# A decode step of two attention and two feed-forward layers: one K transfer of each layer in uneven rows

## The chip, the core and the metric

The kernel runs on one core of a Trainium2 chip. A core has five engines with their own instruction streams: PE (TensorE, the matrix unit), DVE (VectorE), ACT (ScalarE), POOL (GpSimd) and SP (SyncE), which here only issues transfers. Sixteen DMA engines move data from the chip's memory into the core's on-chip memory, which has 128 rows (partitions). Matmul results go to a separate accumulator memory, PSUM; its tiles are called `pS` and `pO` here.

The metric is the device time of one execution in microseconds, the median over several runs.

## The reference

One token goes through attention, a feed-forward block, and both once more with the same weights and the same caches. Cut to what is computed:

```python
def _A_ref(x, k_cache, v_cache, wq, wo):          # x: 1 x 1 x 512
    B, Sq, D = x.shape
    H, Dh = 32, 128                                # caches: 1 x 32 x 4096 x 128
    q = (x @ wq).reshape(B, Sq, H, Dh)             # then heads first
    scores = jnp.einsum("bhqd,bhkd->bhqk", q, k_cache) * (Dh ** -0.5)
    p = _softmax(scores, axis=-1)
    o = jnp.einsum("bhqk,bhkd->bhqd", p, v_cache)
    return o.reshape(B, Sq, H * Dh) @ wo           # heads back in place first

def _B_ref(x, w1, b1, w2, b2):                     # 512 -> 1376 -> 512
    h = jnp.einsum("bsd,df->bsf", x, w1) + b1
    h = _gelu(h)
    return jnp.einsum("bsf,fd->bsd", h, w2) + b2

x = A_x
x = x + _A_ref(_layernorm(x, axis=-1), A_k_cache, A_v_cache, A_wq, A_wo)
x = x + _B_ref(_layernorm(x, axis=-1), B_w1, B_b1, B_w2, B_b2)
x = x + _A_ref(_layernorm(x, axis=-1), A_k_cache, A_v_cache, A_wq, A_wo)
x = x + _B_ref(_layernorm(x, axis=-1), B_w1, B_b1, B_w2, B_b2)
return x
```

All numbers are float32. Each cache holds 67 MB, and each has to be read in both layers, but for the parts that the kernel keeps on the chip between them.

## The kernel before

The 32 heads are treated as `G = 8` groups of `J = 4` heads. The host lays the caches out so that the K of one group, `in_k[g]`, is a block of 128 rows of 16,384 numbers (64 KB a row, 8.39 MB in all), and V likewise. A block is cut along the row into `C = 8` pieces of `NC = 2048` numbers, one for each eighth of the sequence.

**One group.** K is transferred, and `scores` takes it piece by piece: four matmuls for each piece (one for each head), 32 in all, added up in `pS`. `exponentials` and `weights` make the softmax: maximum on DVE, exponential on ACT, a transpose on PE. V is transferred, and `values` runs its 32 matmuls into `pO`. `head_out` multiplies by the group's part of `wo`, and `next_queries` makes the query of the next group from its part of `wq`; both parts come in one transfer of 2 MB (`pair`).

**Where things lie.** One tile, `arena`, holds all that is transferred. Three places of 8.39 MB each, `RING`, take K and V of the groups in turn, so a transfer may begin when the matmuls that read the earlier tenant of its place are done. `PAIR` holds the two weight parts.

**Two layers.** Layer 1 goes through the groups 0 to 7 and ends with the feed-forward block `mlp`. Layer 2 goes back from the groups whose K and V are still on the chip: first two groups that are partly there, and then, in the loop over `n` from 2 to 7, groups 5 to 0. In the last group of each layer K goes in two halves (`HALVES`) and V in four pieces (`LAST`).

**What sets the order.** `load` issues each transfer on SP and keeps it in program order; `matmul` keeps PE's order. SP issues a transfer as soon as its waits are over. The sixteen DMA engines work through what SP has issued. Each transfer counts up one of eight semaphores, `DMAHW0` to `DMAHW7`, taken in turn by SP's transfers and by ACT's three small ones at the start (`xcol`, `b1c`, `b2c`); a transfer also waits for the one before it on its semaphore, where nothing else has waited for that already.

**What the change touches.** `blocks` (line 251) issues the transfers of a K or V and yields its pieces; its argument `pieces` says in how many transfers. It is called with one piece for the whole block, `((0, C),)`, at line 289 for layer 1 (with `g` the group) and at line 361 for layer 2 (with `n`). The profile shows all transfers of `load` at line 70, and all matmuls but the transposes at line 74. A K transfer is shown there as `arena<-in_k`.

Of the kernel before, what the change touches and what calls it, by code (L numbers as in the profile page):

```python
# [23 lines left out]
C = 8  # L24
# [5 lines left out]
NC = 4 * U  # L30
# [12 lines left out]
HALVES = ((0, 4), (4, 8))  # L43
# [7 lines left out]
def decode_layers(ctx: ExitStack, tc: tile.TileContext, x, k, v, w, w1, b1, w2, b2, out):  # L51
    nc = tc.nc
# [12 lines left out]
    def at(first, n):  # L65
        return arena[:, first : first + n]

    def load(first, src):
        t = at(first, src.shape[-1])
        tc.keep_in_program_order(nc.sync.dma_start(t, src))  # L70
        return t

    def matmul(*a, **kw):
        tc.keep_in_program_order(nc.tensor.matmul(*a, **kw))  # L74

    def quarters(first):
        return [at(first + U * j, U) for j in range(4)]

    def part(src, g, a, b):
        return src[g][:, NC * a : NC * b]  # L80

    def of_w(row, i, n):
        return w[row][:, NC * i : NC * (i + n)]

    def by_four(t):
        return t.rearrange("p (j n) -> p j n", j=4)


    wq_t = by_four(load(SHARED, of_w(1, 0, 1)))
    b1c, b2c = ctile("b1c", FB), ctile("b2c", 4)  # L90
    xcol = ctile("xcol", 4)
# [71 lines left out]
    def scores(z, c, kt):  # L163
        for j in range(J):
            matmul(pS[32 * j : 32 * j + C, :], z[:, j, C - 1 - c : 2 * C - 1 - c], kt[j],
                   start=(c == 0), stop=(c == C - 1))

    def exponentials(sc, nsc):
        nc.vector.tensor_reduce(mx[:, 0:1], pS, axis=AX.X, op=ALU.max)  # L169
        mt, m, bias = small("mt", 32), small("m"), small("bias", 32)  # L170
        nc.vector.transpose(mt, mx)  # L171
        nc.vector.tensor_reduce(m, mt[:, :C], axis=AX.X, op=ALU.max)
        nc.vector.tensor_scalar(mb[:, :C], m.to_broadcast([P, C]), nsc, None, op0=ALU.mult)  # L173
        nc.vector.transpose(bias, mb)  # L174
        p = at(SCRATCH, U)
        nc.scalar.activation(p, pS, AF.Exp, bias=bias[:, 0:1], scale=sc, accum_out=ls[:, 0:1])  # L176
        return p

    def weights(p):
        for b in range(4):  # L180
            tc.keep_in_program_order(nc.tensor.transpose(  # L181
                pT[:, b].rearrange("p j r -> p (j r)"), p[:, P * b : P * (b + 1)], ident))
        pt = work.tile([P, J, C, 4], F32, name="pt")
        nc.vector.tensor_copy(pt, pT[:, :, :, :C].rearrange("p b j c -> p j c b"))  # L184
        lt, l, lr, rl = small("mt", 32), small("l"), small("lr", 32), small("rl")
        nc.vector.transpose(lt, ls)  # L186
        nc.vector.tensor_reduce(l, lt[:, :C], axis=AX.X, op=ALU.add)
        nc.vector.tensor_copy(lb, l.to_broadcast([P, 32]))
        nc.vector.transpose(lr, lb)
        nc.vector.reciprocal(rl, lr[:, 0:1])  # L190
        return pt, rl

    def values(i, pt, vt, c):
        for j in range(J):
            matmul(pO[32 * j : 32 * j + 4, :], pt[:, j, c, :], vt[j],
                   start=(i == 0), stop=(i == C - 1))

    def head_out(rl, wt):
        ot = at(SCRATCH, U)
        nc.vector.transpose(ot, pO)  # L200
        o, on = small("o", 4), small("on", 4)
        own = at(SCRATCH, 4 * 129).rearrange("p (b q) -> p b q", q=129)[:, :, :P]
        own = own.rearrange("p b (d q) -> p d b q", q=32)[:, :, :, 0]
        nc.vector.tensor_reduce(o, own, axis=AX.X, op=ALU.add)  # L204
        nc.vector.tensor_scalar(on, o, rl, None, op0=ALU.mult)  # L205
        for d in range(4):
            for j in range(J):
                matmul(pS[32 * j : 32 * j + 1, :P], on[:, d : d + 1], wt[:, d, P * j : P * (j + 1)],
                       start=(d == 0), stop=(d == 3))
        return of_32(turned(pS), 4)  # L210
# [31 lines left out]
    def load_w1(first, a, b):  # L242
        load(first + W1C * a, w1[:, W1C * a : W1C * b])

    def load_w2(first, a, b):
        load(first + U * a, w2[:, U * a : U * b])
# [1 line left out]
    def in_rows(first, n, rows):  # L248
        return [at(first + n * i, n) for i in range(rows)]

    def blocks(src, g, home, pieces=((0, C),)):
        for a, b in pieces:
            load(home + NC * a, part(src, g, a, b))
            for c in range(a, b):
                yield c, quarters(home + NC * c)

# [16 lines left out]
    def next_queries(n, xs, negm, wt):  # L273
        for c in range(4):
            query_block(c, xs, wt)
        return queries(n, negm)

    def add_up(acc, own):
        t = small("acc", 4)
        nc.vector.scalar_tensor_tensor(t, own, 1.0, acc, op0=ALU.mult, op1=ALU.add)  # L280
        return t
# [4 lines left out]
    for g in range(G):  # L286
        final = g == G - 1
        k_home, v_home = RING[2 * g % 3], RING[(2 * g + 1) % 3]
        for c, t in blocks(k, g, k_home, HALVES if final else ((0, C),)):
            scores(z, c, t)  # L290
        pt, rl = weights(exponentials(sc, nsc))
        if final:
            wo_t = by_four(load(PAIR, of_w(g % 2, g, 1)))
        for c, t in blocks(v, g, v_home, LAST if final else ((0, C),)):
            values(c, pt, t, c)
            if g == G - 2:
                for j in range(J):
                    i = 4 * c + j - KEPT_V // U
                    if i >= 0:
                        nc.scalar.copy(pK[i], t[j])  # L300
        if final:
            for i in range(3):
                load_w1(SHARED, i, i + 1)
            own = head_out(rl, wo_t)
            load_w1(SHARED, 3, 4)
        else:
            pair = load(PAIR, of_w(g % 2, g, 2))
            acc = add_up(acc, head_out(rl, by_four(pair[:, :NC])))
            wq_t = by_four(pair[:, NC:])
            z = next_queries(g + 1, xs, negm, wq_t)  # L310
# [7 lines left out]
    g = G - 2  # L318
# [26 lines left out]
    for i, first in enumerate([SHARED + 8 * U, SHARED + 9 * U] + [PAIR + U * j for j in range(4)]):  # L345
        t = at(first, U)
# [11 lines left out]
    for n in range(2, G):  # L358
        g, final = G - 1 - n, n == G - 1
        k_home, v_home = homes[(2 * n - 1) % 3], homes[2 * n % 3]  # L360
        for c, t in blocks(k, g, k_home, HALVES if final else ((0, C),)):
            scores(z, c, t)
        pt, rl = weights(exponentials(sc, nsc))
        if final:
            wo_t = by_four(load(PAIR, of_w(g % 2, g, 1)))
        for c, t in blocks(v, g, v_home, LAST if final else ((0, 6), (6, 8)) if n == 2 else ((0, C),)):
            values(c, pt, t, c)
        if final:
            for a, b in HALVES_W1:
                load_w1(A_AT, a, b)  # L370
            for a, b in W2_AT_END:
                load_w2(A_AT + 11 * U, a, b)
            own = head_out(rl, wo_t)
        else:
            pair = load(PAIR, of_w(g % 2, g - 1, 2))
            acc = add_up(acc, head_out(rl, by_four(pair[:, NC:])))
            z = next_queries(n + 1, xs, negm, by_four(pair[:, :NC]))
# [47 lines left out]
```

## Time and profile before

| | |
|---|---|
| median of 3 runs | 683.48 us (683.07 to 687.48) |
| the profiled execution | 684.24 us |
| its span, from the first instruction to the last | 682.5 us |
| read from the chip's memory in the span | 286.14 MB, 419 GB/s |
| TensorE clock granted, mean | 0.772 |
| matmuls of `scores` (`pS<-arena,zq`) | 1024, 144.1 us busy, 725 ns each |
| matmuls of `values` (`pO<-arena,pt`) | 1024, 146.5 us busy, 734 ns each |
| idle time of TensorE ahead of `scores`, mostly until a K lands | 160.3 us |

How to read the profile: the page begins with each engine's busy time and share of the span (PEld is TensorE's weight load, which overlaps PE). Then come 40 equal slices of the span: a digit is the busy share of a slice in tenths, DMA is the mean of the core's sixteen DMA engines, and GB/s is what they moved. The queues follow: q1 is what SP issues, q10 what ACT issues, q8 and q14 fetch instructions. The chain is followed back from the last instruction: at each step to what released it. In it, "another core or an unknown queue" stands for a wait that no instruction of the core ended; in the middle of this kernel's layers the operation that comes behind it is one that reads transferred data. All times in the views are in microseconds from the start of the span. The clock granted is a share of TensorE's full clock.

### The profile page before, as it was taken

To read this page: it belongs to the slowest core of one execution; us is meant where nothing else is said; L and a number is where in the kernel's file an instruction comes from. 1 tells how busy PE (TensorE), PEld (TensorE's weight loads), DVE (VectorE), ACT (ScalarE), POOL (GpSimd) and SP (SyncE) were. 2 spreads that over 40 slices of the span, in tenths; PEclk is the share of its full clock that TensorE was granted. 3 is DMA by queue.
4 is the path that set the end of the run, shared out by engine and by line. 5 is a ranking of instruction groups with operands and counts; after the bars stand their busy time and mean duration, and the time that the engine had idled before them with its cause. 6 is when DMAs were issued, how large, how long until landed. Compare 5 with 4: busy or idle time off the path is not lost.

```text
span 682.5 us, 7552 instructions
## 1 busy us (share of the span) xinstructions
PE 351.9 (52%) x3440; PEld 99.5 (15%) x3440; DVE 83.6 (12%) x346; ACT 21.9 (3%) x47; POOL 3.6 (1%) x17
## 2 busy tenths in 40 slices
PE   1543663545524655156565878625525643366554
PEld 0111110111111111012012222111111110111112
DVE  1011100111001100111012121110011101111012
ACT  0010000000000000001000010000000000000000
POOL 0000000000000000000000000000000000000000
PEclk9968766797678866787768898886577866877778
DMA  9999999999999999999999999999999999999995
GB/s 369 431 430 443 442 443 435 424 437 430 427 430 408 450 430 431 434 419 434 428 397 337 375 433 423 427 443 447 438 431 404 458 431 438 424 419 429 427 416 225
DMA packets 10976, 286.63 MB, mean 420 GB/s; under 512 B 1728, under 2 KB 1728, under 8 KB 3008
## 3 DMA queue, kind: packets, MB, share of 16 engines
q1 hardware_dynamic: 10512, 286.14, 98.1%
q8 instruction: 27, 0.44, 0.3%
q10 hardware_dynamic: 432, 0.01, 0.0%
q14 instruction: 5, 0.04, 0.0%
HBM read 286.14 MB, written 0.00 MB: 419 GB/s over the span
## 4 chain that ended last, share of the span: by engine, by line
PE 39%; DMA 26%; another core or an unknown queue 25%; DVE 6%; ACT 1%; issue 1%; SPq 0%; ACTq 0%; DVEq 0%
PE pO L74 20%; PE pS L74 18%; DMA arena<-in_v 10%; DMA arena<-in_w 8%; DMA arena<-in_k 7%; DVE arena L200 1%; ACT arena L176 1%; PE pO L181 1%; DVE mx L169 1%; DMA xcol<-in_x 1%; DVE on L205 0%; DVE mb L173 0%; DVE mt L171 0%; DVE o L204 0%
## 5 line engine op out<-in xcount | busy, mean ns | idle before, releaser
L74 PE MATMUL pS<-arena,zq 128*8 128x512 f32 x1024 | 144.1, 725 | 160.3 <-DMA arena<-in_k 159.1
L74 PE MATMUL pO<-arena,pt 128*4 128x512 f32 x1024 | 146.5, 734 | 84.6 <-DMA arena<-in_v 83.8
L74 PEld LDWEIGHTS pS<-arena,zq 128*8 128x8 f32 x1024 | 30.0, 102 | 263.8 <-issue 248.3
L74 PEld LDWEIGHTS pO<-arena,pt 128*4 128x4 f32 x1024 | 28.1, 98 | 193.0 <-issue 186.6
L169 DVE TENSOR_REDUCE mx<-pS 128x1 f32<-128x512 f32 x16 | 11.1, 692 | 294.0 <-PE pS L74 294.0
L200 DVE STREAM_TRANSPOSE arena<-pO 128x512 f32<-128x512 f32 x16 | 11.5, 717 | 225.7 <-PE pO L74 225.7
L181 PE MATMUL pO<-ident,arena 128*128 128x128 f32 x64 | 13.7, 351 | 44.7 <-ACT arena L176 44.7
L176 ACT ACTIVATE arena<-pS,bias,sc 128x512 f32<-128x512 f32 x16 | 12.4, 777 | 544.6 <-DVE bias L174 544.6
L74 PE MATMUL pO<-arena,xs 128*2 128x128 f32 (+1 forms) x576 | 24.4, 307 | 9.5 <-DVE xs L126 8.3
L74 PE MATMUL pS<-arena,on 128*1 128x128 f32 x512 | 16.9, 272 | 21.2 <-DVE on L205 21.2
L181 PEld LDWEIGHTS pO<-ident,arena 128*128 128x128 f32 x64 | 8.8, 174 | 58.8 <-ACT arena L176 53.8
L74 PEld LDWEIGHTS pS<-arena,on 128*1 128x1 f32 x512 | 11.6, 83 | 36.6 <-DVE on L205 36.1
L74 PEld LDWEIGHTS pO<-arena,xs 128*2 128x2 f32 x576 | 14.5, 87 | 13.1 <-issue 9.2
L74 PE MATMUL pS<-arena,gelu_g 128*1 128x128 f32 x176 | 8.6, 355 | 7.2 <-DVE gelu_g L235 4.3
L119 DVE STREAM_TRANSPOSE turned<-pS 128x128 f32<-128x128 f32 x18 | 5.7, 317 | 30.5 <-PE pS L74 30.5
L74 PEld LDWEIGHTS pS<-arena,gelu_g 128*1 128x1 f32 x176 | 4.8, 102 | 11.5 <-DVE gelu_g L235 5.6
L119 DVE STREAM_TRANSPOSE turned<-pO 128x128 f32<-128x128 f32 x16 | 5.1, 316 | 5.5 <-PE pO L74 4.7
L186 DVE STREAM_TRANSPOSE mt<-ls 128x32 f32<-128x32 f32 x16 | 3.4, 211 | 17.4 <-ACT arena L176 17.4
L184 DVE COPY pt<-pO 128x128 f32<-128x128 f32 x16 | 4.3, 267 | 2.0 <-PE pO L181 2.0
L173 DVE TENSOR_SCALAR mb<-m,nsc 128x8 f32<-128x8 f32 x16 | 3.7, 231 | 0.6
L205 DVE TENSOR_SCALAR on<-o,rl 128x4 f32<-128x4 f32 x16 | 3.7, 229 | 0.6
L159 DVE SCALAR_TENSOR_TENSOR zq<-turned,negm 128x4 f32<-128x4 f32 x16 | 3.6, 226 | 0.5
(58 smaller groups left out, 54.6 us busy)
## 6 DMA issues: line engine op xcount, KB each, us to landing
arena<-in_w SPq DMA_DIRECT2D x13, 2048.0 KB, 36.1
arena<-in_k SPq DMA_DIRECT2D x5, 4096.0 KB, 46.0
arena<-in_v SPq DMA_DIRECT2D x2, 4096.0 KB, 24.1
arena<-in_w SPq DMA_DIRECT2D x6, 1024.0 KB, 14.8
arena<-in_v SPq DMA_DIRECT2D x3, 2048.0 KB, 28.5
arena<-in_v SPq DMA_DIRECT2D x1, 6144.0 KB, 32.2
arena<-in_v SPq DMA_DIRECT2D x4, 1024.0 KB, 31.5
arena<-in_w SPq DMA_DIRECT2D x4, 688.0 KB, 30.4
```

Of the source, the lines that this page charges most:

```text
L74: tc.keep_in_program_order(nc.tensor.matmul(*a, **kw))
L119: nc.vector.transpose(t, src[:, :P])
L159: nc.vector.scalar_tensor_tensor(z[:, :, C - 1], of_32(qt, J, 1), negm, of_32(qt, J), op0=ALU.mult, op1=ALU.add)
L169: nc.vector.tensor_reduce(mx[:, 0:1], pS, axis=AX.X, op=ALU.max)
L173: nc.vector.tensor_scalar(mb[:, :C], m.to_broadcast([P, C]), nsc, None, op0=ALU.mult)
L176: nc.scalar.activation(p, pS, AF.Exp, bias=bias[:, 0:1], scale=sc, accum_out=ls[:, 0:1])
L181: tc.keep_in_program_order(nc.tensor.transpose(pT[:, b].rearrange("p j r -> p (j r)"), p[:, P * b : P * (b + 1)], ident))
L184: nc.vector.tensor_copy(pt, pT[:, :, :, :C].rearrange("p b j c -> p j c b"))
L186: nc.vector.transpose(lt, ls)
L200: nc.vector.transpose(ot, pO)
L205: nc.vector.tensor_scalar(on, o, rl, None, op0=ALU.mult)
```

## The change

A new helper, `load_uneven`, issues one block of rows as three transfers: rows 0 to 111, rows 112 to 119 and rows 120 to 127. `blocks` gets an argument `uneven`; with it, every piece but the first goes through the new helper. It is used once in each layer: for K of group 1 in layer 1, and for K of `n == 3` (group 4) in layer 2. These K now go in two halves of 4.19 MB, the first as one transfer of 128 rows, the second in the three. A row of a half is 8192 numbers, 32 KB. The change is described as one by which eight DMA engines carry two rows more than the others: 112 rows are seven for each of sixteen engines, and the two transfers of 8 rows are one row each for eight of them, and the same eight in both.

```diff
+    def load_uneven(first, src):
+
+        t = at(first, src.shape[-1])
+        for a, b in ((0, 112), (112, 120), (120, 128)):
+            tc.keep_in_program_order(nc.sync.dma_start(t[a:b], src[a:b]))
...
-    def blocks(src, g, home, pieces=((0, C),)):
+    def blocks(src, g, home, pieces=((0, C),), uneven=False):
         for a, b in pieces:
-            load(home + NC * a, part(src, g, a, b))
+            (load_uneven if uneven and a else load)(home + NC * a, part(src, g, a, b))
             for c in range(a, b):
                 yield c, quarters(home + NC * c)
...
-        for c, t in blocks(k, g, k_home, HALVES if final else ((0, C),)):
+        for c, t in blocks(k, g, k_home, HALVES if final or g == 1 else ((0, C),), g == 1):
...
-        for c, t in blocks(k, g, k_home, HALVES if final else ((0, C),)):
+        for c, t in blocks(k, g, k_home, HALVES if final or n == 3 else ((0, C),), n == 3):
```

What moves, on SP at the start of layer 1. Each row is a transfer, its size and the semaphores that it waits for; the second row is K of group 0, the fifth K of group 1, then come V of group 1, the weights, and K and V of group 2. Before:

```order
L70 DMA arena<-in_w 128x2048
L70 DMA arena<-in_k 128x16384
L70 DMA arena<-in_v 128x16384 [waits DMAHW1_49,PE_49]
L70 DMA arena<-in_w 128x4096
L70 DMA arena<-in_k 128x16384
L70 DMA arena<-in_v 128x16384 [waits DMAHW4_49,DMAHW0_49,PE_49]
L70 DMA arena<-in_w 128x4096 [waits DMAHW6_49,PE_49]
L70 DMA arena<-in_k 128x16384 [waits DMAHW5_49,DMAHW2_49]
L70 DMA arena<-in_v 128x16384 [waits DMAHW7_49,DMAHW3_49,PE_49]
```

After:

```order
L70 DMA arena<-in_w 128x2048
L70 DMA arena<-in_k 128x16384
L70 DMA arena<-in_v 128x16384 [waits DMAHW1_49,PE_49]
L70 DMA arena<-in_w 128x4096
L70 DMA arena<-in_k 128x8192
L77 DMA arena<-in_k 112x8192 [waits DMAHW0_49]
L77 DMA arena<-in_k 8x8192
L77 DMA arena<-in_k 8x8192 [waits DMAHW2_49]
L70 DMA arena<-in_v 128x16384 [waits DMAHW4_49,DMAHW3_49,PE_49]
L70 DMA arena<-in_w 128x4096 [waits DMAHW6_49,PE_49]
L70 DMA arena<-in_k 128x16384 [waits DMAHW5_49]
L70 DMA arena<-in_v 128x16384 [waits DMAHW2_49,DMAHW1_49,DMAHW7_49,DMAHW0_49,PE_49]
```

One K row has become four. With three more transfers in the turn of the eight semaphores, the waits for `DMAHW2` and `DMAHW3` (those of ACT's `b1c` and `b2c`) have moved forward: from K and V of group 2 to the second 8-row transfer and to V of group 1. The wait for `DMAHW0`, which the first weights count up, has moved from V of group 1 to the 112 rows.

On SP in layer 2, from K of `n == 3` on. Before:

```order
L70 DMA arena<-in_w 128x4096 [waits DMAHW2_49,DMAHW1_49,Activation_49]
L70 DMA arena<-in_k 128x16384
L70 DMA arena<-in_v 128x16384 [waits DMAHW6_49,PE_49]
L70 DMA arena<-in_w 128x4096 [waits DMAHW1_49,PE_49]
L70 DMA arena<-in_k 128x16384 [waits DMAHW7_49,DMAHW0_49]
```

After:

```order
L70 DMA arena<-in_w 128x4096 [waits DMAHW5_49,DMAHW4_49,Activation_49]
L70 DMA arena<-in_k 128x8192
L77 DMA arena<-in_k 112x8192
L77 DMA arena<-in_k 8x8192 x2
L70 DMA arena<-in_v 128x16384 [waits DMAHW1_49,PE_49]
L70 DMA arena<-in_w 128x4096 [waits DMAHW4_49,DMAHW2_49,PE_49]
L70 DMA arena<-in_k 128x16384 [waits DMAHW3_49]
```

The added transfers wait for nothing here, and V waits for as many things as before.

On PE, the scores of group 1 in layer 1: the queries, the 32 matmuls of `scores` and the transposes behind them. Before:

```order
L74 MATMUL pO<-arena,xs 2x128 x16
L74 MATMUL pS<-arena,zq_92 8x512 [waits DMAHW7_49,DVE_49]
L74 MATMUL pS<-arena,zq_92 8x512 x31
L181 MATMUL pO<-ident,arena 128x128 [waits Activation_49]
L181 MATMUL pO<-ident,arena 128x128 x3
```

After:

```order
L80 MATMUL pO<-arena,xs 2x128 x16
L80 MATMUL pS<-arena,zq_92 8x512 [waits DMAHW7_49,DVE_49]
L80 MATMUL pS<-arena,zq_92 8x512 x15
L80 MATMUL pS<-arena,zq_92 8x512 [waits DMAHW2_49,DMAHW1_49,DMAHW0_49]
L80 MATMUL pS<-arena,zq_92 8x512 x15
L187 MATMUL pO<-ident,arena 128x128 [waits Activation_49]
L187 MATMUL pO<-ident,arena 128x128 x3
```

The first sixteen matmuls now wait for the first half alone, and the other sixteen for all three transfers of the second half.

## The prediction

> **What bounds the kernel now.** I read the page first: the shares of the engines, the 40 slices of the DMA engines, the queues and the chain.
>
> ```profile
> span 682.5 us, 7552 instructions
> ...
> PE 351.9 (52%) x3440; PEld 99.5 (15%) x3440; DVE 83.6 (12%) x346; ACT 21.9 (3%) x47; POOL 3.6 (1%) x17
> ...
> DMA  9999999999999999999999999999999999999995
> GB/s 369 431 430 443 442 443 435 424 437 430 427 430 408 450 430 431 434 419 434 428 397 337 375 433 423 427 443 447 438 431 404 458 431 438 424 419 429 427 416 225
> ...
> q1 hardware_dynamic: 10512, 286.14, 98.1%
> q8 instruction: 27, 0.44, 0.3%
> ...
> PE 39%; DMA 26%; another core or an unknown queue 25%; DVE 6%; ACT 1%; issue 1%; SPq 0%; ACTq 0%; DVEq 0%
> ```
>
> TensorE is busy for half of the span. The sixteen DMA engines are full in all slices but the last, and queue q1, which SP feeds, has 98.1% of them. The chain gives PE the largest share, but a chain counts a matmul as work even where the next one waits for data anyway. So I asked next for the busy time by stretch: the two around the first K transfer to be split, one behind them, and most of layer 2.
>
> ```profile
> core 0: us, PE busy (x) PEld busy (x) DVE busy (x) ACT busy (x) POOL busy (x), PEclk, DMA share, GB/s
> 12.00:56.00 44.00, 20.47 (x132) 4.53 (x132) 2.75 (x12) 2.15 (x3) 0.00 (x0) 0.84 1.00 429
> 58.00:100.00 42.00, 21.66 (x176) 5.30 (x164) 3.68 (x16) 0.87 (x2) 0.00 (x0) 0.67 1.03 442
> 100.00:144.00 44.00, 22.04 (x216) 6.43 (x220) 5.87 (x21) 0.87 (x2) 0.00 (x0) 0.73 1.00 430
> 466.00:630.00 164.00, 85.69 (x784) 23.65 (x784) 18.45 (x70) 3.47 (x8) 0.00 (x0) 0.72 1.00 429
> ```
>
> A share of 1.00 at 429 to 430 GB/s is a ceiling: 430 / 16 = 26.9 GB/s for each DMA engine. (The 442 beside a share of 1.03 is an effect of where a stretch is cut.) One group of a layer is K and V of 8.39 MB each and 2.1 MB of weights, 18.9 MB, or 43.9 us at that rate. The chain in order of time shows the same period; here is one group, and then the end.
>
> ```profile
> 59.15 11.27 another core or an unknown queue
> 70.56 9.47 PE pS L74 x64
> 80.05 0.70 DVE mx L169
> ...
> 83.85 5.93 another core or an unknown queue
> 89.92 10.02 PE pO L74 x64
> ...
> 133.49 8.73 PE pO L74 x64
> ...
> 510.28 9.76 PE pS L74 x64
> ...
> 645.01 31.12 DMA arena<-in_w
> 676.17 3.21 PE pS L74 x56
> ```
>
> From one V's matmuls (89.92) to the next (133.49) pass 43.6 us, the 43.9 us of the bytes. The gaps of 11.27 and 5.93 us are TensorE waiting for a landing. The kernel ends 6.3 us after the last weights land (676.17 to 682.5). How deep the queue is, SP's own rows tell:
>
> ```profile
> 9.10 0.46 SPq L70 DMA_DIRECT2D arena<-in_k  x1
> 35.28 0.33 SPq L70 DMA_DIRECT2D arena<-in_v  x1
> ...
> 59.63 0.38 SPq L70 DMA_DIRECT2D arena<-in_k  x1
> 80.04 0.33 SPq L70 DMA_DIRECT2D arena<-in_v  x1
> ...
> 449.83 0.38 SPq L70 DMA_DIRECT2D arena<-in_k  x1
> ```
>
> The V issued at 80.04 is used from 133.49, 53.4 us later; its own 8.39 MB take 19.5 us, so 33.9 us of other transfers stand ahead of it. Therefore nothing that happens on SP or TensorE within some 30 us matters, and the time is the time of the slowest DMA engine: each works down its own share of every transfer, and only the drain at the end of a layer makes them wait for each other.
>
> **The change, part by part.**
>
> *Halving the transfer.* TensorE may begin on the first half 9.7 us earlier and has about 4.7 us less to do once the whole K is there. This frees SP's next V earlier, into a queue 33.9 us deep: worth 0. If that cover were gone it would be worth up to 4.7 us in each layer.
>
> *Six more issues on SP,* three in each layer, at 0.33 to 0.46 us: 2.4 us in all. SP waits far longer than that, so they cost 0:
>
> ```profile
> SPq L70 <- DMA arena<-in_w: 227.7, 16, 35.4
> ```
>
> *Waits that the new semaphore order brings.* By the order shown above, the second 8-row transfer of layer 1 now waits for semaphore 2 and the V behind it for semaphore 3. These are the first ones that the ACT queue's small loads use, b1c and b2c.
>
> ```profile
> 1.16 0.46 ACTq L93 DMA_DIRECT2D b1c<-in_b  x1
> 1.65 0.45 ACTq L94 DMA_DIRECT2D b2c<-in_b  x1
> ...
> b1c<-in_b ACTq DMA_DIRECT2D x1, 5.5 KB, 24.3
> b2c<-in_b ACTq DMA_DIRECT2D x1, 2.0 KB, 44.7
> ```
>
> They land at 1.16 + 24.3 = 25.5 and 1.65 + 44.7 = 46.4 us. So the V goes out at 46.4 instead of 35.28. Behind it on SP stand weights and the K that went out at 59.63, so nothing else is held. The K that is split lands at about 70.5 (its matmuls start at 70.56), so 24 us of queue are still ahead of the V: 0. If the cover were gone the price would be 11.1 us, once. In layer 2 the added transfers bring no wait of their own.
>
> *The uneven rows.* This is the only term on the path. A row of the half is 32 KB: 32,768 B / 26.9 GB/s = 1.22 us of one engine. Evenly spread, the half costs every engine 8 rows, 9.7 us. After the change the 112 rows cost 7 rows, 8.5 us, and eight engines carry two rows more. What a transfer of only 8 rows costs these eight, no row of before shows, since all transfers on q1 have 128 rows. The bounds:
> - Low: the rate belongs to the engine, wherever it writes. Two rows cost 2.4 us; the eight engines end at 8.5 + 2.4 = 10.9 us, 1.2 us late, and the other eight 1.2 us early.
> - High: the rate belongs to the place written. In every transfer before, a sixteenth of the destination took in a sixteenth of 430 GB/s, never more. If eight adjacent rows are such a sixteenth, then one 8-row transfer takes 8 x 1.22 = 9.7 us on whichever engines, the two 19.5 us, and the eight engines end at 28.0 us, 18.3 us late.
>
> I take two sixteenths for eight adjacent rows: 4.9 us for an 8-row transfer, 9.7 us for both, end at 18.3 us, 8.5 us late. It is nearer to the high end, because the one thing that the rows of before do show of 8 rows of destination is 26.9 GB/s for 8 rows together, while an engine with its neighbours writing into the same few rows is shown nowhere.
>
> The Trainium skill has a rule for this that speaks against the change: SBUF — State Buffer, Door 1: The DMA port swizzle, says that four adjacent partitions share one of sixteen ports at about 27 GB/s, so eight adjacent ones reach two ports. By its figure the two transfers would cost 9.6 us, and the sum below would stand; by a rate of the engine alone it would be that of the first rival. No row of this trace can show it, since full transfers use all partitions. And on which engines: the Trainium skill, DMA: Bandwidth & Descriptors, Why a DMA increments its semaphore by 16 and not by 1, puts an 8-row transfer on the eight lowest-numbered engines; the profile does not name engines.
>
> *What of this reaches the end.* Some engines are late already, since instruction fetches fall on them: 27 on q8 take 0.3% of sixteen engines' span, 0.003 x 16 x 682.5 / 27 = 1.2 us each. If the other eight engines had all the 13 or 14 of a layer, the latest of them would have two, 2.4 us; if the same eight, the lead is 0. I take the middle, 1.2 us. So a layer ends 8.5 - 1.2 = 7.3 us later. The drain at the end of each layer makes all wait for the slowest, so the two layers add.
>
> **Sum.** 2 x 7.3 = 14.6 us; the other parts 0. The profiled execution took 684.24 us (the span and 1.74 us around it), 0.76 us above the median of the three runs, 683.48. Against the median: 698.1 us, 2.1% slower. This case's own range is 693 to 705: low, with a lead of three fetches, 3.6 us, 683.5 + 2 x 4.9; high, where the engines whose usual rows these are write there as well (five rows share the rate of one instead of four, 2 x 1.2 us more in each layer) and the lead is 0, 683.5 + 2 x 10.9.
>
> **The rivals.**
> 1. *The rate is the engine's, and the late engines are the other eight* (not slower). Place: the drain at the end of each layer. The eight get 1.2 us more each layer, the late ones 1.2 us less: 683.5 - 2.4 = 681.1 us. For it: 26.9 GB/s on each of sixteen, with nothing in the rows to say that the destination sets it, and fetches that do make engines unequal. Against it: fetches are worth only 1.2 us each, so the others may not be behind at all. It decides if an 8-row transfer takes less than about 1.8 us on its engines: then two rows more are at most the lead of 2.4 us and a little.
> 2. *The rate is the engine's, and the eight are those that are late already.* 2 x 1.2 us more: 685.9 us. The same rows speak for it.
> 3. *The change does not do what it says,* and the 16 rows spread over all sixteen engines, or the lag is taken up before the drain: 683.5 us. Against it: a queue that is never empty gives a late engine no time to catch up.
> 4. *Eight adjacent rows are one sixteenth.* 18.3 us late in each layer, less 1.2: 683.5 + 34.2 = 717.7 us.
>
> **How the numbers follow.** Chances: the forecast 0.54, rival 1 0.22, rival 2 0.10, rival 3 0.08, rival 4 0.06. A measurement of this kernel can tell about 1%, 6.8 us, from no change. Rivals 1 to 3 lie within it, 0.40. Slower by over 1% are the forecast and rival 4, 0.60, less 0.02 for a forecast that comes out small: 0.58. Faster by over 1% needs 6.8 us, which no row offers: 0.02. The range reaches from rival 1, with 0.3 us of spread, 680.8, to the upper part of the forecast, 705; it leaves out rival 4 and a tenth of the forecast, about 0.12.
>
> **What would show it.** For the forecast: the first matmuls of the split K's second half start some 8 us later than 70.56 and 510.28 against the bytes ahead of them; the moved GB/s fall below 400 in the slices around 50 to 75 and 490 to 515 us; the last weights' matmuls start near 691 (676.17 + 14.6) instead of 676.17. Against it: the rate stays at 430 there, and all landings keep their distance of 43.9 us. The halving is right if TensorE begins the first half early and V's start does not move; the new wait is right if V goes out at 46 us and its matmuls still start near 90, plus the lag. I am wrong above all if a few rows can be written by many engines at full rate.

## The result and the profile after

The changed kernel takes 717.53 us (median of 6 runs, 716.11 to 721.33) beside 684.46 us for the kernel before (6 runs): the ratio is 1.0473, with a 95% interval of 1.0446 to 1.0501. It is 4.7% slower; forecast were 698.1 us and a range up to 705.

The page of the changed kernel, the span, the DMA engines' busy tenths, what they moved, and SP's queue:

```profile
span 714.3 us, 7560 instructions
...
DMA  9999999999999999999988999999999999999995
GB/s 411 412 409 318 235 414 457 416 437 434 426 441 417 447 434 419 440 409 439 425 352 308 387 443 431 417 319 234 413 443 440 423 433 434 438 426 417 434 410 206
...
q1 hardware_dynamic: 10832, 286.14, 97.7%
```

The DMA engines are as busy as before and move the same 286.14 MB, but twice the rate falls: to 318 and 235 GB/s in the fourth and fifth slice (54 to 89 us), and to 319 and 234 in two slices of layer 2 (464 to 500 us). Those are the two places where the uneven halves go. Elsewhere the rate is about that of before. So a DMA engine can be busy and slow at once, and the busy share does not show it; the GB/s beside it do.

The same stretches of layer 1, as busy times with DMA share and GB/s at the end of each row, before:

```profile
58.00:72.00 14.00, 2.60 (x52) 1.15 (x44) 1.02 (x4) 0.00 (x0) 0.00 (x0) 0.63 1.02 441
72.00:84.00 12.00, 9.09 (x64) 2.31 (x56) 2.38 (x10) 0.87 (x2) 0.00 (x0) 0.78 1.01 437
```

and after:

```profile
58.00:72.00 14.00, 6.59 (x80) 1.96 (x70) 1.02 (x4) 0.00 (x0) 0.00 (x0) 0.88 1.03 261
72.00:84.00 12.00, 0.00 (x0) 0.00 (x0) 0.00 (x0) 0.00 (x0) 0.00 (x0) 0.52 1.06 169
```

The first stretch is mostly the 112 rows, the second the two 8-row transfers. Both are slow: 261 and 169 GB/s. (A packet is counted in the stretch in which it starts, so where the share is above 1.00 the GB/s is too high by about that factor.) The forecast had only the second one slow.

TensorE's instructions after, in order of time: start, length, and in brackets the idle time ahead and what ended it.

```profile
62.11 5.30 PE L80 MATMUL pS<-arena,zq 128*8 128x512 f32 x32 [2.82 <-DMA arena<-in_k]
86.05 5.28 PE L80 MATMUL pS<-arena,zq 128*8 128x512 f32 x32 [18.63 <-DMA arena<-in_k]
...
105.17 5.09 PE L80 MATMUL pO<-arena,pt 128*4 128x512 f32 x24 [10.44 <-DMA arena<-in_v]
```

The first half of K is there at 62, the second at 86, and V's matmuls start at 105.17 instead of 89.92: layer 1 is 15.3 us late from here on. The span grew by 31.8 us, so layer 2 adds 16.5.

SP's issues at the start, and two of its waits:

```profile
9.10 0.46 SPq L70 DMA_DIRECT2D arena<-in_k  x1
9.61 16.02 SPq L77 DMA_DIRECT2D arena<-in_k  x3
46.26 0.36 SPq L70 DMA_DIRECT2D arena<-in_v  x1
```

```profile
SPq L70 <- DMA b2c<-in_b: 20.6, 1, 20.6
...
SPq L77 <- DMA b1c<-in_b: 14.9, 1, 14.9
```

The waits of the new semaphore order came as read from the order: V goes out at 46.26.

### The profile page after: what moved, and what is told of

It reads as the page before. It is cut to its first block, busy times and chain, and to the rows that moved or that the text cites. A ratio compares the mean times of both kernels' runs of the same rounds, so it can differ in the third digit from the quotient of the medians.

```text
span 714.3 us, 7560 instructions
## 1 busy us (share of the span) xinstructions
PE 351.9 (49%) x3440; PEld 100.4 (14%) x3440; DVE 83.4 (12%) x346; ACT 21.9 (3%) x47; POOL 3.6 (1%) x17
## 3 DMA queue, kind: packets, MB, share of 16 engines
q1 hardware_dynamic: 10832, 286.14, 97.7%
HBM read 286.14 MB, written 0.00 MB: 401 GB/s over the span
## 4 chain that ended last, share of the span: by engine, by line
PE 39%; another core or an unknown queue 29%; DMA 22%; DVE 6%; issue 1%; ACT 1%; SPq 1%; ACTq 0%; DVEq 0%
PE pO L80 19%; PE pS L80 18%; DMA arena<-in_v 10%; DMA arena<-in_w 7%; DMA arena<-in_k 5%; DVE arena L206 1%; ACT arena L182 1%; DVE mx L175 1%; PE pO L187 1%; DMA xcol<-in_x 1%; SPq L70 1%; DVE on L211 0%; DVE mb L179 0%; DVE mt L177 0%
## 5 line engine op out<-in xcount | busy, mean ns | idle before, releaser
L80 PE MATMUL pO<-arena,pt 128*4 128x512 f32 x1024 | 143.8, 723 | 96.0 <-DMA arena<-in_v 95.2
L80 PE MATMUL pO<-arena,xs 128*2 128x128 f32 (+1 forms) x576 | 27.2, 331 | 8.9 <-DVE xs L132 7.6
L80 PE MATMUL pS<-arena,on 128*1 128x128 f32 x512 | 18.5, 290 | 21.2 <-DVE on L211 21.2
```

## The experiments

All kernels are the changed one with another `load_uneven`, unless the diff says otherwise. Theories: A, a few neighbouring rows of the destination, called a place below, take in only so much, whoever writes; B, the unequal engines; C, transfers of few rows are slow as such; S, the source.

In the table, a row is 32 KB of the split half of layer 1. Its times are the packet records of the trace: one record for each row, start and duration. The large part is the sum of the medians of its rows on an engine. The records do not name the engine.

```
kernel              large part, us        small rows, us each    ratio to before, 95%
before              (1.21 a row)          none                   1
changed             112 rows: 14.2        4.5                    1.0473 (1.0446 to 1.0501)
e1_halves           128 rows: 9.7         none                   1.0004 (0.9982 to 1.0026)
e2_112_16           112 rows: 14.1        4.4                    1.0373 (1.0323 to 1.0423)
e3_own               96 rows: 13.8        1.2 to 1.5             1.0303 (1.0269 to 1.0337)
e4_adjacent          96 rows: 14.0        4.2                    1.0596 (1.0567 to 1.0625)
e5_place_apart       96 rows: 13.8        1.2 to 1.4             1.0304 (1.0233 to 1.0375)
e6_source_apart      96 rows: 13.7        4.4 to 4.5             1.0620 (1.0558 to 1.0681)
e7_other_half        96 rows: 14.0        2.6                    1.0446 (1.0404 to 1.0488)
e8_64_64             none                 2.4 to 2.6             1.0371 (1.0326 to 1.0416)
e9_two_at_a_place   112 rows: 15.1        2.4 to 2.5             1.0334 (1.0268 to 1.0400)
e11_eight_apart      none                 2.2 to 2.5             1.0352 (1.0312 to 1.0393)
```

### Halving alone

```diff
-        for a, b in ((0, 112), (112, 120), (120, 128)):
-            tc.keep_in_program_order(nc.sync.dma_start(t[a:b], src[a:b]))
+        tc.keep_in_program_order(nc.sync.dma_start(t, src))
```

> The two K transfers go in two halves of 128 rows each, no uneven rows. All theories that blame the rows of the second half (where they are written, or how few there are) expect the time of the kernel before, within 2 us. The rival that the halving itself or the earlier start of the matmuls costs something expects a good part of the 33 us, 10 us or more.

685.04 us beside 685.94: no difference. TensorE's rows of this kernel:

```profile
60.67 3.62 PE L79 MATMUL pS<-arena,zq 128*8 128x512 f32 x32 [1.56 <-DMA arena<-in_k]
70.55 6.07 PE L79 MATMUL pS<-arena,zq 128*8 128x512 f32 x32 [6.26 <-DMA arena<-in_k]
...
90.00 5.31 PE L79 MATMUL pO<-arena,pt 128*4 128x512 f32 x36 [9.50 <-DMA arena<-in_v]
```

The halves are 9.9 us apart here (23.9 in the changed kernel), and V starts at 90.00, as before (89.92). Halving is worth nothing, and all of the loss lies in the uneven rows.

### Without an imbalance: 112 and 16 rows

```diff
-        for a, b in ((0, 112), (112, 120), (120, 128)):
+        for a, b in ((0, 112), (112, 128)):
```

> The second half goes as 112 and 16 rows: 7 and 1 rows for each of sixteen engines, so no engine has more bytes than another. Theory A (a few adjacent rows of destination take in only about 27 GB/s for each four of them, whichever engines write): the 112 rows stay as slow as in the changed kernel, where the trace has about 14 us for them instead of 8.5, and the 16 rows take 4.9 instead of 1.2 us: 9 us a layer, 18 us in all, about 702 us. Theory B (the imbalance of the engines is the cause: eight engines with more rows): no imbalance, time as before within 2 us.

710.44 us, 24.5 more than before: theory B falls, since no engine has more bytes than another here. Theory A gave the direction and fell short by 8 us. V starts 12 us late in layer 1, and the rows account, by their medians, for 14.1 + 4.4 - 9.7 = 8.8. Most of the other 3 us lie in the slowest engine: the last row ends at 81.8 us and most by 78.5, where in `e1_halves` it is 70.0 and 68.8. Behind the half nothing is lost: V's matmuls follow those of the second half by 19.1 us, in `e1_halves` by 19.4. The two stretches:

```profile
58.00:72.00 14.00, 6.98 (x64) 1.63 (x52) 1.02 (x4) 0.00 (x0) 0.00 (x0) 0.73 1.01 263
72.00:84.00 12.00, 1.05 (x8) 0.31 (x12) 0.00 (x0) 0.00 (x0) 0.00 (x0) 0.50 1.03 257
```

and its V in TensorE's instructions:

```profile
102.03 8.22 PE L80 MATMUL pO<-arena,pt 128*4 128x512 f32 x60 [8.98 <-DMA arena<-in_v]
```

The first stretch is that of the changed kernel (261 GB/s): the 112 rows are slow by themselves, without any 8-row transfer behind them.

### Eight rows, four apart or adjacent

```diff
-        for a, b in ((0, 112), (112, 120), (120, 128)):
-            tc.keep_in_program_order(nc.sync.dma_start(t[a:b], src[a:b]))
+        for r in [slice(32, 128)] + [slice(i, 32, 4) for i in range(4)]:
+            tc.keep_in_program_order(nc.sync.dma_start(t[r], src[r]))
```

> The second half goes as rows 32 to 127 (96 rows) and four transfers of 8 rows, each taking every fourth row of 0 to 31. If the same eight engines take all four, they have ten rows and the others six, an imbalance of 2.4 us a layer, larger than in the change. Theory A: eight rows four apart lie in eight different places of four, so they go at the engines' rate, 1.2 us a row. Then only the imbalance and whatever the 96 rows lose are left: 5 to 15 us in all, 689 to 699 us. Theory C (8-row transfers are slow whatever rows they write, 4.4 us a row): as slow as the next kernel, or more than 715 us.

For the second kernel the four small transfers are `slice(8 * i, 8 * i + 8)`:

> As the kernel with every fourth row, but the four 8-row transfers take adjacent rows: 0 to 7, 8 to 15, 16 to 23, 24 to 31. Same bytes, same number of rows for each engine. Theory A: 4.4 us a row as in the changed kernel's trace, 17.6 us for the four instead of 4.9, so 25 us more than the kernel with every fourth row, about 715 to 725 us. Theory C: the same time as the kernel with every fourth row, within 3 us.

706.33 and 727.38 us: 21 us between two kernels with the same bytes for each engine, so theory C falls. The first is 7 us above the range that theory A was given, since the 96 rows took 13.8 us instead of six rows' 7.3, more than had been allowed for. The stretches of the one with rows four apart:

```profile
58.00:72.00 14.00, 6.37 (x76) 1.81 (x64) 1.02 (x4) 0.00 (x0) 0.00 (x0) 0.88 1.00 226
72.00:84.00 12.00, 4.10 (x28) 0.97 (x32) 0.00 (x0) 0.00 (x0) 0.00 (x0) 0.57 1.06 429
```

and of the one with adjacent rows:

```profile
58.00:72.00 14.00, 5.32 (x32) 1.13 (x32) 0.23 (x1) 0.00 (x0) 0.00 (x0) 0.88 1.01 226
72.00:84.00 12.00, 0.00 (x0) 0.00 (x0) 0.00 (x0) 0.00 (x0) 0.00 (x0) 0.53 1.20 150
84.00:100.00 16.00, 5.77 (x32) 1.09 (x32) 1.51 (x5) 0.21 (x1) 0.00 (x0) 0.61 0.84 283
```

The 96 rows ahead are equally slow in both (226 GB/s). Then the small transfers four rows apart run at the full 429 GB/s together with the V on the other engines, and the adjacent ones at 150, which at a share of 1.20 stands for about 125. Four rows apart, eight rows cost their engines 1.2 us each, as in a full transfer.

### Source or destination

In the first kernel each small transfer reads adjacent rows and writes every fourth; in the second it reads every fourth and writes adjacent ones:

```diff
+        for to, of in [(slice(32, 128),) * 2] + [(slice(i, 32, 4), slice(8 * i, 8 * i + 8)) for i in range(4)]:
+            tc.keep_in_program_order(nc.sync.dma_start(t[to], src[of]))
```

> As e3_own and e4_adjacent, with source and destination taken apart: each 8-row transfer reads adjacent rows of the source and writes every fourth of rows 0 to 31. Rows 0 to 31 of that half of K lie in another order, so the output is not the reference's. Theory A (the destination: a few adjacent rows take in little): as e3_own, 1.2 us a row, 706 us. Theory S (the source: adjacent rows of the source are read slowly by eight engines at once): as e4_adjacent, 4.2 us a row, 727 us.

> The other way about: each 8-row transfer reads every fourth of source rows 0 to 31 and writes adjacent rows. The rows of that half of K lie in another order, so the output is not the reference's. Theory A: as e4_adjacent, 727 us. Theory S: as e3_own, 706 us.

704.56 and 727.81 us. Written apart it is the time of `e3_own`, written side by side that of `e4_adjacent`, whatever is read: for these transfers the destination decides, and theory S falls. For the large part, source and destination were not taken apart.

### Where the owner writes too

```diff
+        for r in [slice(0, 96)] + [slice(96 + i, 128, 4) for i in range(4)]:
+            tc.keep_in_program_order(nc.sync.dma_start(t[r], src[r]))
```

> As e3_own, but rows 0 to 95 go in one transfer and the four 8-row transfers take every fourth row of 96 to 127, source and destination alike. Theory A, with places of four rows, each of them usually written by one engine: if these places belong to the eight engines that are not busy with the 8-row transfers, each has two writers here, its own engine (with the V behind) and one of the eight: about 2.4 us a row, 5 us a layer more than e3_own, 712 to 718 us. Theory S: as e3_own, 706 us, since the source rows are as far apart.

715.37 us, as theory A had it, and 2.6 us a row instead of 1.2. The stretch of the small transfers:

```profile
72.00:84.00 12.00, 0.00 (x0) 0.00 (x0) 0.00 (x0) 0.00 (x0) 0.00 (x0) 0.50 1.09 259
```

The small rows fit two writers at a place that get half of the rate each: rows 96 to 127 would then belong, in a full transfer, to engines other than the eight of a small one, and rows 0 to 31 to those eight. The V rows beside them, 64 KB each, take 5.1 to 5.7 us in the packet records instead of 2.4, but that does not show who writes where: in `e9_two_at_a_place` below, where the small rows are in 0 to 15, V's take 4.7 to 5.2 us too.

### Halves of the rows

```diff
+        for r in (slice(0, 64), slice(64, 128)):
+            tc.keep_in_program_order(nc.sync.dma_start(t[r], src[r]))
```

> The second half goes as rows 0 to 63 and rows 64 to 127: two full transfers, four rows for each of sixteen engines in each, no imbalance. Theory A: 64 rows are half of the places, two engines at each: 2.4 us a row, 19.4 us instead of 9.7 for the half, about 19 us more in all, 705 us. Theory S or an imbalance: the source is read four rows apart as in a transfer of 128 rows, and time is as before, within 2 us.

710.06 us, 5 more than theory A was given: 2.4 to 2.6 us a row, the rate of two engines at each place, with full use of sixteen engines and no imbalance. The stretch shows about half of the rate:

```profile
58.00:72.00 14.00, 7.16 (x92) 2.24 (x80) 1.02 (x4) 0.00 (x0) 0.00 (x0) 0.76 1.06 219
```

### Two writers instead of four

```diff
-        for a, b in ((0, 112), (112, 120), (120, 128)):
-            tc.keep_in_program_order(nc.sync.dma_start(t[a:b], src[a:b]))
+        for r in (slice(16, 128), slice(0, 16, 2), slice(1, 16, 2)):
+            tc.keep_in_program_order(nc.sync.dma_start(t[r], src[r]))
```

> As the changed kernel, 112 rows and two transfers of 8, with the same bytes for each engine; but the 112 are rows 16 to 127, and the 8-row transfers take every other row of 0 to 15, so two engines instead of four write at each place of four rows. Theory A with a price that follows the number of writers at a place: 2.5 us instead of 4.4 for each of these rows, 4 us a layer less than the changed kernel, about 709 us; the 112 rows stay at about 14 us. A theory in which only the number of rows and engines counts: 717 us as the changed kernel.

709.84 us, 2.4 to 2.5 us a row: with the bytes of the change on every engine, the price follows the number of writers at a place. One writer costs 1.2 (`e3_own`), two 2.5, four 4.2 to 4.5.

### One layer

```diff
-        for c, t in blocks(k, g, k_home, HALVES if final or n == 3 else ((0, C),), n == 3):
+        for c, t in blocks(k, g, k_home, HALVES if final else ((0, C),)):
```

> The changed kernel with the uneven half in layer 1 alone; layer 2 as before. If each layer pays for itself, since all engines are waited for at its end: half of the 33 us, about 701 us. If the lag of layer 1 were taken up later, or the two layers' lags did not add: less than 692 or more than 708 us.

700.55 us beside 686.46, a ratio of 1.0205 (1.0160 to 1.0250), of the 1.0473 for both layers. That is 14.1 us, and V starts 14.0 us late in layer 1 of its profile (103.93 against 89.92). Layer 1 pays its share and layer 2 adds its own; nothing is taken up later.

### Which rows share a place

```diff
+        for r in [slice(i, 128, 8) for i in range(8)]:
+            tc.keep_in_program_order(nc.sync.dma_start(t[r], src[r]))
```

> The second half goes as eight transfers of 16 rows, each taking every eighth row: one row for each of sixteen engines in each, no imbalance, and no two rows of a transfer within eight of each other. If a place is just four adjacent rows, each row has its place for itself: 1.2 us a row, time as before within 3 us. If rows 32 apart belong to the same place too, two engines write at each: 2.5 us a row, 20 us for the half instead of 9.7, about 706 us, as with 64 and 64 rows.

709.77 us and 2.2 to 2.5 us a row. No two rows of such a transfer are closer than eight, and still they go as if each shared its place with another one. Rows 4 to 28 apart did not share in `e3_own`, so the partner lies 32 rows or more away. The second expectation had 32; this run does not tell 32 from more.

## Why the prediction was wrong

**What bounds the kernel** was right: the time is that of the slowest DMA engine. A second half that comes 15.5 us late (86.05 against 70.55 in `e1_halves`) delays V by 15.3 us and ends up in the time, layer by layer (`e10_layer_1`).

**Halving and the new waits** cost nothing, as forecast: `e1_halves` is at 1.0004, and V went out at 46.26 (46.4 forecast), while the engines were still full with the K ahead of it. The six more issues were not tried alone.

**The failing step: "After the change the 112 rows cost 7 rows, 8.5 us".** They took 14 us, in the changed kernel and in `e2_112_16`, where nothing uneven follows. The price of an engine's row in a full transfer was carried over to a transfer with seven rows an engine, and no reason was given. The prediction did ask what the destination does to the 8 rows, and did not ask it of the 112. What the runs showed in its place: of the transfers on sixteen engines only that of all 128 rows moved at 1.2 us a row; 112, 96, 64 and every eighth row took 2.0 to 2.6. This term alone is 5.6 us a layer, 11 of the 19 us missing. That two engines write at each place fits 64 and every eighth row; why 112 and 96 rows are slow is not shown, and is taken up under what stays open.

**The two 8-row transfers: right.** The prediction put 4.9 us on each, between bounds of 1.2 and 9.7; a row took 4.5 us in the changed kernel, 4.2 to 4.5 in the experiments with adjacent rows. The Trainium skill, SBUF — State Buffer, Door 1: The DMA port swizzle, has ports of four adjacent rows that rows 32 apart share too. The runs agree with that: rows four apart go at full rate (`e3_own`), 64 rows, and every eighth row, at half (`e8_64_64`, `e11_eight_apart`). Its 27 GB/s for a port is met with two writers (two rows of 32 KB in 2.5 us are 26) and somewhat low with four: eight adjacent rows in 4.2 us are 62 GB/s for two of them. Counting the ports that a transfer reaches does not price the 112 rows: in its map, rows 0 to 111 reach all sixteen.

**The lead of 1.2 us a layer** that the fetches were to give back did not show. It rested on eight engines that are late beside eight that go on, "1.2 us early". In the changed kernel the other eight did not go on: while the 8-row transfers ran, their 64 KB rows of V took 8.0 to 9.0 us instead of 2.4, twice a 32 KB row of the small transfers. The first half is used 1.4 us later, too, than in `e1_halves` (62.11 against 60.67). The lead and this make 5 us in both layers; of the 3 us that remain, one is the kernel before, which ran at 684.46 beside the changed one and not at 683.48, and the rest is not assigned.

**Rival 4 gave 717.7 us, and is wrong all the same.** It asked for 9.7 us for an 8-row transfer, which is twice what the rows took; the rest of the loss lies in the 112 rows. **Rivals 1 and 2** fall, since the rate is not the engine's wherever it writes. **Rival 3** falls as well: in the packet records of the changed kernel eight small rows and eight rows of V are under way at 79 us, in `e4_adjacent` from 78 to 88 us, so the small transfers do not spread over sixteen engines; and the lag was not taken up (`e10_layer_1`).

**A place misread:** the split K of layer 2 is the one whose matmuls start at 466.68 in the chain before, and not the one issued at 449.83 and used from 510.28. No term rested on it, but the marks named for layer 2 did: the rate fell from 464 us on, not from 490.

**What stays open.** While a few places were crowded, the eight engines that carried V were slowed to the pace of the others. A 64 KB row of V took about twice what a 32 KB small row took: 8.0 to 9.0 us in the changed kernel, 8.1 to 8.5 in `e4_adjacent`, 4.7 to 5.2 in `e9_two_at_a_place`, and 2.4 in `e3_own` once the 96 rows were done. In `e4_adjacent` and `e9_two_at_a_place` these engines write at other places, if `e7_other_half` is read rightly. What holds them up was not tried.

The same may slow the 112 and 96 rows. If their rows are dealt out in order, six or seven neighbours to an engine, some place has two writers at every step; if all sixteen engines keep the pace of that place, an estimate from the 2.4 us of two writers is 6 x 2.4 = 14.4 us for 96 rows (13.8 measured) and 7 x 2.4 = 16.8 for 112 (14.1 measured), which fits the 96 and is too much for the 112. How the rows are dealt out was not tried, nor whether the source has a part in it, nor which engines were late before.

## What to carry to other kernels

Of the transfers on sixteen engines here, only that of all 128 rows went at full rate; splitting it by rows costs even where every engine keeps the same bytes (64 and 64 rows: 2.6 instead of 1.2 us a row, 3.7% of this kernel from two halves of 4 MB). Split by columns instead: two halves of 128 rows cost nothing. Where fewer rows must go, count the writers at each place (four adjacent rows and the four that lie 32 further), and take rows four apart at places that no other transfer is writing (`e3_own` against `e7_other_half`); and judge a DMA-bound stretch by its GB/s, since the engines look busy all the same.

## What the runs showed of the hardware that was not expected

- 112 rows on sixteen engines moved at 261 to 263 GB/s, 96 rows at 226, 64 rows at 219, beside 441 for 128 rows: a transfer with one row in eight left out is 40% slower.
- Crowded places slow all sixteen engines, and not only the eight that write there: in `e4_adjacent` eight engines with adjacent rows take 62 GB/s, and the other eight, with 64 KB rows of V in 8.3 us, no more (63), where sixteen moved 437 GB/s before.
